# Global tokens in row-by-batch order, and the last output block in two column halves

## The chip, the cores and the metric

The kernel runs on one core of a Trainium2 chip. The metric is the device time of one execution in microseconds (us). Before the change three runs took 361.5, 361.63 and 361.71 us; their median is 361.63 us.

## The reference

Attention with a window, and a gated product behind it, for 8 batches of 8 heads, 512 local and 32 global tokens, head size 64 (so D = 512 columns). All is float32.

```python
out_g = softmax(scale * q_g @ [k_g, k_l].T) @ [v_g, v_l]            # 32 global tokens see all 544
out_l = softmax([scale * q_l @ k_g.T, band(scale * q_l @ k_l.T)]) @ [v_g, v_l]   # |i - j| <= 32
x = concat([out_g, out_l], tokens), heads side by side              # (8, 544, 512)
gate = sigmoid(causal convolution of x over tokens, 5 taps for each column)
out = ((gate * (x @ w_val)) @ w_out)                                # (8, 544, 512)
```

## The kernel before

Attention works on 32 units, each a batch and a pair of heads (`NU`, 128 columns of x). Its results stand transposed: 128 columns of x on the partitions, tokens along the free dimension. For the local tokens each batch has four such tiles of 512 tokens. The global tokens of all 8 batches are collected in `xgT` ([128, 4 column tiles, 8 batches, 4 + 32 tokens]; the four extra places hold zeros, for the causal taps) and are worked on once, at the very end, as one block of 8 x 32 = 256 tokens.

The function `moe` does the gated product: first product `g1` (x by `w_val`, for each of four output tiles e over four input tiles t), `gv` (times the gate, on DVE), `gh` and `gl` (the value split in a rounded high part and a rest, for float32 precision from three fast products), and second product `g2` (by `w_out`), which turns the result round: 128 tokens on the partitions, 512 columns in one PSUM bank. Each of `g1` and `g2` issues three matmuls for a step (high x high, high x low, low x high). `ob` copies a finished bank to SBUF and `st` stores it. `moe` is called for the eight batches (keys 0 to 7) and last with key `g` for the global tokens; there `g2` has two blocks r = 0, 1 of 128 tokens.

Before the call with key `g`, `wg_part` makes its inputs for each column tile from `xgT`, on DVE: `high` (a cast, `gxh`), `low` (a subtraction, `gxl`) and `conv` (`gconv`: one product with the first tap, then four scalar_tensor_tensor steps). They write the tiles `xgh`, `xgl` and `gateg`, each 128 x 256, through the views `hv`, `lv` and `acc`. Then `sigg` takes the sigmoid of the four gates on ACT.

Every task's place in its engine's queue is fixed by the table `ORDER`, written out by hand; a `Plan` gives the tasks their PSUM banks (the number behind @ in the table). The table ends

```
... g2.g.0.3 g2.g.1.0@5 st.7.3 g2.g.1.1 ob.g.0 g2.g.1.2 st.g.0 g2.g.1.3 ob.g.1 st.g.1
```

A store with key `g` was four DMAs, one for each batch in the block (32 tokens by 512 columns, 64 KB), in turn on the queues of SP and ACT.

Of the kernel before, what the change touches and what calls it, by code (L numbers as in the profile page):

```python
# [8 lines left out]
F32 = mybir.dt.float32  # L9
# [8 lines left out]
B, H, SL, SG, D = 8, 8, 512, 32, 64  # L18
DM = H * D
KW = 5  # L20
P = 128
NDT = DM // P
NU = B * NDT
# [294 lines left out]
def attention_moe(ctx, tc, qk, vw, maskd, w_val, convT, w_out, out):  # L318
    nc = tc.nc
    V, A, G, T = nc.vector, nc.scalar, nc.gpsimd, nc.tensor  # L320

    cp = ctx.enter_context(tc.tile_pool(name="cp", bufs=1))
    sb = ctx.enter_context(tc.tile_pool(name="sb", bufs=2))
    ps = ctx.enter_context(tc.tile_pool(name="ps", bufs=1, space=PSUM))

    plan = Plan()
    psum = ps.tile([P, 8, SL], F32, name="psum")

    def bank(key):
        return psum[:, plan.at[key][0], :]  # L330
# [23 lines left out]
    wvh, wvl, woh, wol = (cp.tile([P, NDT, DM], F32R, name=n) for n in ("wvh", "wvl", "woh", "wol"))  # L354
# [46 lines left out]
    def copy(name, out, in_):  # L401
        eng = plan.tasks[name].eng
        if eng == "ACT":
            A.copy(out, in_)  # L404
        else:
            (V if eng == "DVE" else G).tensor_copy(out, in_)
# [3 lines left out]
    def on_pe(ins):  # L410
        last_pe[:] = [ins.ins]
# [291 lines left out]
    gates, xs_h, xs_l = {}, {}, {}  # L703
# [3 lines left out]
    def moe(key, n, x0, deps_x, deps_gate, before, store):  # L707

        box = {}
        last = before  # L710

        def g1(e, t):
            xh, xl = xs_h[x0 + t], xs_l[x0 + t]
            if t == 0:
                box["pv", e] = bank(f"g1.{key}.{e}")[:, :n]
            for q, (w, x) in enumerate(((wvh, xh), (wvh, xl), (wvl, xh))):
                on_pe(T.matmul(box["pv", e], w[:, e, t * P:t * P + P], x, start=(t == 0 and q == 0),  # L717
                         stop=(t == NDT - 1 and q == 2)))

        def gv(e):  # L720
            if e == 0:
                box["gh"] = sb.tile([P, NDT, n], F32R, tag="gh", name=f"gh{key}", bufs=1)
                box["gl"] = sb.tile([P, NDT, n], F32R, tag="gl", name=f"gl{key}", bufs=1)
            box["gv", e] = sb.tile([P, n], F32, tag="gv", name=f"gv{key}_{e}")
            V.tensor_tensor(out=box["gv", e], in0=box["pv", e], in1=gates[x0 + e], op=ALU.mult)

        def gh(e):
            copy(f"gh.{key}.{e}", box["gh"][:, e, :], box["gv", e])

        def gl(e):  # L730
            V.tensor_tensor(out=box["gl"][:, e, :], in0=box["gv", e], in1=box["gh"][:, e, :].bitcast(F32),
                            op=ALU.subtract)

        def g2(r, e):
            if e == 0:
                box["po", r] = bank(f"g2.{key}.{r}")
            rs = slice(r * P, r * P + P)
            for q, (g, w) in enumerate(((box["gh"], woh), (box["gh"], wol), (box["gl"], woh))):
                on_pe(T.matmul(box["po", r], g[:, e, rs], w[:, e, :], start=(e == 0 and q == 0),  # L739
                         stop=(e == NDT - 1 and q == 2)))  # L740

        def ob(r):
            box["ob", r] = sb.tile([P, DM], F32, tag="ob", name=f"ob{key}_{r}")
            if (key, r) == ("g", n // P - 1):
                A.copy(box["ob", r][:, :DM // 2], box["po", r][:, :DM // 2])
                V.tensor_copy(box["ob", r][:, DM // 2:], box["po", r][:, DM // 2:])
            else:
                copy(f"ob.{key}.{r}", box["ob", r], box["po", r])

        part = 693 if n == 512 else 356  # L750
        early = [f"pc{u}.{KW - 1}" for u in range(NPC)] if key == 0 else []
        for e in range(NDT):
            for t in range(NDT):
                name = f"g1.{key}.{e}.{t}"
                plan.add(name, "PE", part, lambda e=e, t=t: g1(e, t), [last, f"w{e}"] + deps_x(t) + early,
                         take=[("bank", name[:-2])] if t == 0 else [],
                         give=[("xh", x0 + t), ("xl", x0 + t)] if e == NDT - 1 else [])
                last = name
            plan.add(f"gv.{key}.{e}", "DVE", 601 if n == 512 else 334, lambda e=e: gv(e),
                     [last] + deps_gate(e) + ([f"gv.{key}.{e - 1}"] if e else []),  # L760
                     take=[("gv", f"{key}.{e}")] + ([("g", key)] if e == 0 else []),
                     give=[("bank", f"g1.{key}.{e}"), ("gate", x0 + e)])
            plan.add(f"gh.{key}.{e}", (("ACT", 520 if n == 512 else 385), ("DVE", 335 if n == 512 else 205)), 0, lambda e=e: gh(e),
                     [f"gv.{key}.{e}"], lock=True)
            plan.add(f"gl.{key}.{e}", "DVE", 600 if n == 512 else 338, lambda e=e: gl(e), [f"gh.{key}.{e}"], 
                     give=[("gv", f"{key}.{e}")], lock=True)
        for r in range(n // P):
            for e in range(NDT):
                name = f"g2.{key}.{r}.{e}"
                plan.add(name, "PE", 682, lambda r=r, e=e: g2(r, e),  # L770
                         [last, f"gl.{key}.{e}", f"w{NDT + e}"], take=[("bank", name[:-2])] if e == 0 else [],
                         give=[("g", key)] if (r, e) == (n // P - 1, NDT - 1) else [])
                last = name
            plan.add(f"ob.{key}.{r}", *(("ACT", 350) if (key, r) == ("g", n // P - 1) else ((("ACT", 470), ("DVE", 600)), 0)), lambda r=r: ob(r), [last], take=[("ob", name[3:-2])],
                     give=[("bank", name[:-2])])
            plan.add(f"st.{key}.{r}", "ACT", 800 if key == "g" else 400, lambda r=r: store(r, box["ob", r]), [f"ob.{key}.{r}"])
            plan.add(f"sd.{key}.{r}", "DMA", 620, lambda: None, [f"st.{key}.{r}"], give=[("ob", f"{key}.{r}")])
        return last

    def wg_part(dt):  # L780

        n = B * SG
        src = xgT[:, dt]
        hv, lv, acc = (h[NU + dt].rearrange("p (b q) -> p b q", b=B) for h in (xs_h, xs_l, gates))

        def high():
            V.tensor_copy(hv, src[:, :, KW - 1:])

        def low():
            V.tensor_tensor(out=lv, in0=src[:, :, KW - 1:], in1=hv.bitcast(F32), op=ALU.subtract)  # L790

        def conv():
            V.tensor_scalar(out=acc, in0=src[:, :, 0:SG], scalar1=cw[:, dt, 0:1], scalar2=None, op0=ALU.mult)
            for k in range(1, KW):
                V.scalar_tensor_tensor(out=acc, in0=src[:, :, k:k + SG], scalar=cw[:, dt, k:k + 1], in1=acc,
                                       op0=ALU.mult, op1=ALU.add)

        return high, low, conv
# [40 lines left out]
    for b in range(B):  # L839
# [4 lines left out]
        for h in range(2):  # L844
            n = f"{b}.{h}"
# [16 lines left out]
    for u in range(NU):  # L862
        b, dt = divmod(u, NDT)
# [47 lines left out]
    for b in range(B):  # L911
        units = range(4 * b, 4 * b + 4)
        for u in units:
            plan.add(f"sig{u}", "ACT", 530, lambda u=u: sigmoid(gates[u]),
                     [f"fix{v}" if v < NHF else f"conv{v}.{KW - 2}" for v in units] + ([f"sig{u - 1}"] if u % 4 else []))
        last = moe(b, SL, 4 * b, lambda t, b=b: [f"xl{4 * b + t}"], lambda e, b=b: [f"sig{4 * b + e}"], last,
                   lambda r, o, b=b: A.dma_start(out[b, SG + r * P:SG + r * P + P, :], o))

    def open_g():
        n = B * SG  # L920
        for dt in range(NDT):
            xs_h[NU + dt] = sb.tile([P, n], F32R, tag="xh", name=f"xgh{dt}", bufs=NX)
            xs_l[NU + dt] = sb.tile([P, n], F32R, tag="xl", name=f"xgl{dt}", bufs=NX)
            gates[NU + dt] = sb.tile([P, n], F32, tag="gate", name=f"gateg{dt}", bufs=NX)
        gp.extend(wg_part(dt) for dt in range(NDT))
# [8 lines left out]
    plan.add("sigg", "ACT", 1250, lambda: [sigmoid(gates[NU + dt]) for dt in range(NDT)],  # L934
             [f"gconv{dt}" for dt in range(NDT)])

    def store_g(r, o):
        for s in range(P // SG):
            (A if s % 2 else nc.sync).dma_start(out[r * (P // SG) + s, 0:SG, :], o[s * SG:s * SG + SG, :])

    moe("g", B * SG, NU, lambda t: [f"gxl{t}"], lambda e: ["sigg"], last, store_g)

    with tc.manual_schedule():
# [91 lines left out]
```

## Time and profile before

| | |
|---|---|
| time, median of 3 runs | 361.63 us |
| the profiled execution's own time | 361.64 us |
| its span, from the first to the last instruction | 359.9 us |
| mean granted TensorE clock | 0.994 |
| busy: PE / DVE / ACT | 349.9 / 315.3 / 254.3 us |
| DMA traffic | 66.73 MB, 185 GB/s over the span |

Times in the views count from the start of the span. PE is the matmul engine, DVE the vector engine, ACT the scalar engine; SPq and ACTq are the queues on which SP and ACT issue DMAs. 1.74 us of the execution's time lie outside the span.

### The profile page before, as it was taken

To read this page: it belongs to the slowest core of one execution; us is meant where nothing else is said; L and a number is where in the kernel's file an instruction comes from. 1 tells how busy PE (TensorE), PEld (TensorE's weight loads), DVE (VectorE), ACT (ScalarE), POOL (GpSimd) and SP (SyncE) were. 2 spreads that over 40 slices of the span, in tenths; PEclk is the share of its full clock that TensorE was granted. 3 is DMA by queue.
4 is the path that set the end of the run, shared out by engine and by line. 5 is a ranking of instruction groups with operands and counts; after the bars stand their busy time and mean duration, and the time that the engine had idled before them with its cause. 6 is when DMAs were issued, how large, how long until landed. Compare 5 with 4: busy or idle time off the path is not lost.

```text
span 359.9 us, 14810 instructions
## 1 busy us (share of the span) xinstructions
PE 349.9 (97%) x6331; PEld 280.0 (78%) x6331; DVE 315.3 (88%) x1085; ACT 254.3 (71%) x652; POOL 0.8 (0%) x7
## 2 busy tenths in 40 slices
PE   8899999899999999999999999999999999999995
PEld 4666687778787888788878877888878888888894
DVE  4899999999989899899899997989599696988981
ACT  3899999897897688987788566776659458523131
POOL 0000000000000000000000000000000000000000
PEclk9899999999999999999999999999999999999999
DMA  7995947695675734925666482823854101000223
GB/s 280 400 362 166 359 156 279 209 402 193 226 235 199 276 104 108 391 102 171 221 241 237 159 277 104 262 67 132 283 165 173 62 2 51 13 29 36 112 87 87
DMA packets 17249, 66.73 MB, mean 185 GB/s; under 512 B 1952, under 2 KB 4000, under 8 KB 17184
## 3 DMA queue, kind: packets, MB, share of 16 engines
q1 hardware_dynamic: 12240, 57.12, 45.2%
q10 hardware_dynamic: 4944, 8.67, 6.6%
q8 instruction: 49, 0.80, 0.9%
q14 instruction: 16, 0.13, 0.1%
HBM read 56.87 MB, written 8.91 MB: 183 GB/s over the span
## 4 chain that ended last, share of the span: by engine, by line
PE 81%; ACT 8%; DMA 5%; DVE 3%; issue 1%; SPq 1%; ACTq 0%; DVEq 0%
PE psum L717 25%; PE psum L739 23%; PE psum L603 7%; PE psum L567 7%; PE psum L592 7%; PE psum L632 4%; DMA v<-in_vw_dram 3%; PE psum L531 3%; DMA out_dram<-ob 2%; ACT pm L586 2%; PE psum L493 2%; ACT xs L624 2%; PE psum L511 1%; DVE gate L668 1%; ACT xc L404 1%
## 5 line engine op out<-in xcount | busy, mean ns | idle before, releaser
L586 ACT ACTIVATE pm<-pm,mx 128x128 f32<-128x128 f32 x256 | 80.9, 407 | 25.8 <-DVE mx L579 22.5
L668 DVE SCALAR_TENSOR_TENSOR gate<-xc,cw,gate 128x512 f32<-128x512 f32 x120 | 87.7, 745 | 1.1 <-ACT gate L397 0.4
L579 DVE CUSTOM_DVE_ANT_0 pm<-psum,mask 128x128 f32<-128x128 f32 x256 | 57.4, 285 | 5.2 <-PE psum L567 5.2
L717 PE MATMUL psum<-xh,wvh 128*128 128x512 f32 x128 | 53.8, 421 | 0.0
L739 PE MATMUL psum<-woh,gh 128*128 128x512 f32 x128 | 53.0, 414 | 0.0
L717 PE MATMUL psum<-xl,wvh 128*128 128x512 f32 x128 | 50.6, 396 | 0.0
L717 PE MATMUL psum<-xh,wvl 128*128 128x512 f32 x128 | 50.5, 395 | 0.0
L739 PE MATMUL psum<-woh,gl 128*128 128x512 f32 x128 | 50.2, 392 | 0.0
L739 PE MATMUL psum<-wol,gh 128*128 128x512 f32 x128 | 50.0, 391 | 0.0
L404 ACT COPY pts<-psum 128x512 f32<-128x512 f32 x49 | 28.6, 601 | 16.0 <-PE psum L592 16.0
L592 PE MATMUL psum<-ident,pm 128*128 128x128 f32 x256 | 38.0, 278 | 0.6 <-ACT pm L586 0.3
L567 PE MATMUL psum<-qk 64*32 64x128 f32 x2048 | 38.1, 281 | 0.5 <-ACT pm L586 0.4
L603 PEld LDWEIGHTS psum<-v,pts 128*32 128x32 f32 x2048 | 31.1, 111 | 8.3 <-issue 4.7
L567 PEld LDWEIGHTS psum<-qk 64*32 64x32 f32 x2048 | 30.3, 108 | 8.5 <-issue 3.6
L592 PEld LDWEIGHTS psum<-ident,pm 128*128 128x128 f32 x256 | 29.6, 140 | 9.1 <-ACT pm L586 2.7
L603 PE MATMUL psum<-v,pts 128*32 128x65 f32 x2048 | 34.9, 224 | 1.4 <-DMA v<-in_vw_dram 1.2
L717 PEld LDWEIGHTS psum<-xh,wvl 128*128 128x128 f32 x128 | 24.0, 188 | 5.6 <-issue 0.2
L739 PEld LDWEIGHTS psum<-woh,gl 128*128 128x128 f32 x128 | 24.0, 188 | 5.3
L717 PEld LDWEIGHTS psum<-xh,wvh 128*128 128x128 f32 x128 | 24.3, 190 | 4.5 <-DVE xl L664 0.2
L717 PEld LDWEIGHTS psum<-xl,wvh 128*128 128x128 f32 x128 | 24.2, 189 | 4.1 <-issue 0.2
L739 PEld LDWEIGHTS psum<-woh,gh 128*128 128x128 f32 x128 | 24.2, 189 | 4.0 <-issue 0.2
L739 PEld LDWEIGHTS psum<-wol,gh 128*128 128x128 f32 x128 | 24.2, 189 | 3.9
(111 smaller groups left out, 554.0 us busy)
## 6 DMA issues: line engine op xcount, KB each, us to landing
v<-in_vw_dram SPq DMA_DIRECT2D x32, 975.0 KB, 6.7
qk<-in_qk_dram SPq DMA_DIRECT2D x32, 624.0 KB, 5.0
out_dram<-ob ACTq DMA_DIRECT2D x32, 256.0 KB, 2.2
wraw<-in_w_val_dram SPq DMA_DIRECT2D x4, 512.0 KB, 12.3
wraw<-in_w_out_dram SPq DMA_DIRECT2D x4, 512.0 KB, 4.1
mask<-in_mask_dram SPq DMA_DIRECT2D x1, 256.0 KB, 4.6
out_dram<-obg SPq DMA_DIRECT2D x4, 64.0 KB, 1.7
out_dram<-obg ACTq DMA_DIRECT2D x4, 64.0 KB, 2.0
```

Of the source, the lines that this page charges most:

```text
L404: A.copy(out, in_)
L493: on_pe(T.matmul(s[h][SG * c:SG * c + SG, cols], qkt[rows, SL + SG * h:SL + SG * h + SG], keys, start=True, stop=True))
L531: on_pe(T.matmul(ag[SG * c:SG * c + SG, :], pgt[:k, s, SG * c:SG * c + SG], vt[:k, w, h, :], start=(n == 0), stop=(n == len(steps) - 1)))
L567: on_pe(T.matmul((sx, sy)[h][32 * j:32 * j + 32, i, :], qkt[rows, 32 * m:32 * m + 32], qkt[rows, k0:k0 + P], start=True, stop=True))
L579: V.tensor_tensor_reduce(out=pm[:, h, i, :], in0=s[:, i, :], in1=mask[:, i, :], op0=ALU.add, op1=ALU.min, scale=-SCALE, scalar=3.0e38, acc ...
L586: A.activation(out=pm[:, h, i, :], in_=pm[:, h, i, :], func=AF.Exp, bias=mx[:, c:c + 1], scale=-1.0)
L592: on_pe(T.transpose(pt[:, i, :], pm[:, h, i, :], ident))
L603: on_pe(T.matmul(ax[32 * j:32 * j + 32, h, E1 * i:E1 * i + E1], pts[:, h, i, 32 * j:32 * j + 32], vt[:, block_win(4 * i + j), h, :], start ...
L632: on_pe(T.transpose(xt[:, P * i:P * i + P], xs[:, i].rearrange("p h d -> p (h d)"), ident))
L668: V.scalar_tensor_tensor(out=acc, in0=xc[:, k:k + SL], scalar=cw[:, u % NDT, k:k + 1], in1=acc, op0=ALU.mult, op1=ALU.add)
L717: on_pe(T.matmul(box["pv", e], w[:, e, t * P:t * P + P], x, start=(t == 0 and q == 0), stop=(t == NDT - 1 and q == 2)))
L739: on_pe(T.matmul(box["po", r], g[:, e, rs], w[:, e, :], start=(e == 0 and q == 0), stop=(e == NDT - 1 and q == 2)))
```

## The change

Two things are changed together, both for key `g`.

The 256 global tokens are numbered token by token with the batches inside (q, b) and no longer batch by batch (b, q). The tiles `xgh`, `xgl` and `gateg` keep their size, but DVE now goes through them in steps of 8 elements (32 bytes), since `xgT` is still read batch by batch. One block r of 128 rows of the second product then holds tokens 16r to 16r + 15 of all eight batches, and one DMA of three dimensions (16 tokens, 8 batches, columns) stores it.

The last block (r = 1) is computed by `g2_halves` in two halves of 256 columns, each in its own bank: all twelve products of columns 0 to 255, then all twelve of columns 256 to 511. The first half is copied by DVE to a tile `obg_first` and stored from SP when it is done, the second by ACT and stored from SP. Block r = 0 is stored by one DMA on ACT's queue.

```diff
+        def g2_halves(r, e):
+            if e % (NDT // 2) == 0:
+                used = [plan.at[f"g2.{key}.{i}"][0] for i in (r - 1, r)]
+                spare = next(n for n in (f"g1.{key}.{i}" for i in range(NDT)) if plan.at[n][0] not in used)
+                box["half", e * 2 // NDT] = bank(spare if e else f"g2.{key}.{r}")
+            c, rs = e * 2 // NDT, slice(r * P, r * P + P)
+            for k in range(e * 2 % NDT, e * 2 % NDT + 2):
+                for q, (g, w) in enumerate(((box["gh"], woh), (box["gh"], wol), (box["gl"], woh))):
+                    on_pe(T.matmul(box["half", c][:, :DM // 2], g[:, k, rs], w[:, k, c * DM // 2:(c + 1) * DM // 2],
+                             start=(k == 0 and q == 0), stop=(k == NDT - 1 and q == 2)))
+            if (c, k) == (0, NDT - 1):
+                o = sb.tile([P, DM // 2], F32, tag="gv", name="obg_first")
+                V.tensor_copy(o, box["half", 0][:, :DM // 2])
+                store(r, o, 0)
+
         def g2(r, e):
+            if (key, r) == ("g", n // P - 1):
+                g2_halves(r, e)
+                return
...
         def ob(r):
-            box["ob", r] = sb.tile([P, DM], F32, tag="ob", name=f"ob{key}_{r}")
-            if (key, r) == ("g", n // P - 1):
-                A.copy(box["ob", r][:, :DM // 2], box["po", r][:, :DM // 2])
-                V.tensor_copy(box["ob", r][:, DM // 2:], box["po", r][:, DM // 2:])
+            last_part = (key, r) == ("g", n // P - 1)
+            o = box["ob", r] = sb.tile([P, DM // 2 if last_part else DM], F32, tag="ob", name=f"ob{key}_{r}")
+            if last_part:
+                A.copy(o, box["half", 1][:, :DM // 2])
...
-        hv, lv, acc = (h[NU + dt].rearrange("p (b q) -> p b q", b=B) for h in (xs_h, xs_l, gates))
+        hv, lv, acc = (h[NU + dt].rearrange("p (q b) -> p b q", b=B) for h in (xs_h, xs_l, gates))
...
-    def store_g(r, o):
-        for s in range(P // SG):
-            (A if s % 2 else nc.sync).dma_start(out[r * (P // SG) + s, 0:SG, :], o[s * SG:s * SG + SG, :])
+    def store_g(r, o, c=1):
+        cols = slice(0, DM) if r == 0 else slice(c * DM // 2, (c + 1) * DM // 2)
+        (nc.sync if r else A).dma_start(out[:, P // B * r:P // B * r + P // B, cols].rearrange("b q d -> q b d"), o)
```

The table `ORDER` is the same. Three places show what now stands in the queues; names are those of the program with buffer numbers. First the end of ACT's queue, from the copy of block r = 0 on (`obg`), before (-) and after (+):

```order
-L404 COPY obg_5952<-psum 128x512
-L939 DMA out_dram<-obg_5952 32x512 x2
-L745 COPY obg_5964<-psum 128x256
-L939 DMA out_dram<-obg_5964 32x512 x2
-L1030 UNCONDITIONAL_BRANCH
+L404 COPY obg_5961<-psum 128x512
+L957 DMA out_dram<-obg_5961 16x8x512
+L764 COPY obg_5976<-psum 128x256
+L1048 UNCONDITIONAL_BRANCH
```

ACT issues one DMA where there were four, and none behind its last copy. At the end of SP's queue, behind the last loads of v, the stores of `obg` stand so:

```order
 L416 DMA v_5000<-in_vw_dram 128x1950
-L939 DMA out_dram<-obg_5952 32x512 x2
-L939 DMA out_dram<-obg_5964 32x512 x2
-L1030 UNCONDITIONAL_BRANCH
+L957 DMA out_dram<-obg_first 16x8x256
+L957 DMA out_dram<-obg_5976 16x8x256
+L1048 UNCONDITIONAL_BRANCH
```

SP issues the store of the first half and then that of the second. On DVE no instruction moves in the queue; the last conversions for the global tokens (`gconv2` in the table's words is one product and four scalar_tensor_tensor steps; `gconv3` and `gconv1` follow) now go through 8 x 32 elements where one row of 256 stood, and the last copy writes `obg_first`. The stretch ahead of the gated product, after the change:

```order
L808 TENSOR_TENSOR xgl_5733<-xgT,xgh_5732 128x8x32
L811 TENSOR_SCALAR gateg_5734<-xgT,cw 128x8x32
L813 SCALAR_TENSOR_TENSOR gateg_5734<-xgT,cw,gateg_5734 128x8x32 x4
L811 TENSOR_SCALAR gateg_5728<-xgT,cw 128x8x32
L813 SCALAR_TENSOR_TENSOR gateg_5728<-xgT,cw,gateg_5728 128x8x32 x4
L406 COPY ob_0_5867<-psum 128x512
L725 TENSOR_TENSOR gvg_5889<-psum,gateg_5725 128x256
```

The gated product of the global tokens (`gvg`) stands directly behind these conversions and one copy. On PE the twelve matmuls of 128 x 512 that ended the program are 24 of 128 x 256, each with its own load of weights.

More of the change, by code (lines that the diff above doesn't have):

```diff
@@ L742, in ob @@
         def ob(r):
-            box["ob", r] = sb.tile([P, DM], F32, tag="ob", name=f"ob{key}_{r}")
-            if (key, r) == ("g", n // P - 1):
-                A.copy(box["ob", r][:, :DM // 2], box["po", r][:, :DM // 2])
-                V.tensor_copy(box["ob", r][:, DM // 2:], box["po", r][:, DM // 2:])
+            last_part = (key, r) == ("g", n // P - 1)
+            o = box["ob", r] = sb.tile([P, DM // 2 if last_part else DM], F32, tag="ob", name=f"ob{key}_{r}")
+            if last_part:
+                A.copy(o, box["half", 1][:, :DM // 2])
             else:
-                copy(f"ob.{key}.{r}", box["ob", r], box["po", r])
+                copy(f"ob.{key}.{r}", o, box["po", r])
         part = 693 if n == 512 else 356
```

## The prediction

> **What bounds the kernel now.** I read the page's busy times first, then the chain of waits over the last 30 us, then the timeline of the end, then the stores' landing times. The page, and the chain (start, length, work):
>
> ```profile
> PE 349.9 (97%) x6331; PEld 280.0 (78%) x6331; DVE 315.3 (88%) x1085; ACT 254.3 (71%) x652; POOL 0.8 (0%) x7
> 329.77 3.93 PE psum L717 x17
> 333.70 10.88 PE psum L739 x48
> 344.58 5.69 PE psum L717 x48
> 350.27 5.46 PE psum L739 x24
> 355.73 0.02 issue
> 355.75 0.38 ACT obg L745
> 356.13 0.02 issue
> 356.16 0.42 DVE obg L746
> ```
>
> PE is the bound, and it runs without a gap to 355.73. Behind it comes a tail of 4.2 us in which only the last block is on its way: ACT copies one half, DVE then the other, and four stores go out. These are the rows of the tail:
>
> ```profile
> 355.33 0.39 PE L739 MATMUL psum<-woh,glg 128*128 128x512 f32 x1
> 355.75 0.37 ACT L745 COPY obg<-psum 128x256 f32<-128x256 f32 x1 [2.13 <-PE psum L739]
> 356.16 0.42 DVE L746 COPY obg<-psum 128x256 f32<-128x256 f32 x1 [4.64 <-ACT obg L745]
> 356.61 0.78 SPq L939 DMA_DIRECT2D out_dram<-obg  x2
> 356.62 0.85 ACTq L939 DMA_DIRECT2D out_dram<-obg  x2
> L939 SPq DMA_DIRECT2D out_dram<-obg x2: 315/364/414, 356.6 to 357.0; - x2
> L939 ACTq DMA_DIRECT2D out_dram<-obg x2: 375/408/441, 356.6 to 357.0; - x2
> DMA to landing us min/median/max: 1.6/1.9/2.0
> out_dram<-obg SPq DMA_DIRECT2D x4, 64.0 KB, 1.7
> out_dram<-obg ACTq DMA_DIRECT2D x4, 64.0 KB, 2.0
> SPq L1030 <- DMA out_dram<-obg: 1.4, 2, 1.2
> ```
>
> The two copies don't overlap: DVE waited for ACT, since both write one tile. Then each queue issues two stores one behind the other. ACT's second one starts at 356.62 + 0.85 - 0.44 = 357.03 and lands 2.0 later, at 359.03; SP's starts at 356.98 and lands by 1.7, at 358.7. So ACT's second store ends the program's work, SP waits for it (last row), and 0.87 us of closing steps make the span of 359.9. The profiled execution took 361.64, the median of the runs is 361.63: I count from 361.64 and need no correction.
>
> **The change, part by part.**
>
> *The last block on PE.* Twelve matmuls of 512 columns become 24 of 256. The chain prices both: 24 of L739 take 5.46, so 227 ns each; 48 of L717, which have 256 columns and a weight load each, take 5.69, so 118.5 ns each. 12 x 0.2275 = 2.73 becomes 24 x 0.1185 = 2.84: +0.11 on the path. The twelve start at 355.33 - 11 x 0.2275 = 352.83, so the last of the 24 would start at 352.83 + 23 x 0.1185 = 355.56 and, at the 0.28 that the L717 form takes (row further down), end at 355.84.
>
> *The copies.* ACT's copy stays on the path: 355.84 + 0.02 (issue, as in the chain) = 355.86, and 0.37 later it is 356.23. DVE's copy leaves it, with the issue gap ahead: -0.44. It moves to the first half, which is complete 12 matmuls earlier, at 352.83 + 11 x 0.1185 + 0.28 = 354.41; DVE has nothing to do then (it sat idle for 4.64 ahead of its copy), so it copies until about 354.9 and nothing waits for it but SP's first store, out by 355.3.
>
> *The stores of the last block.* SP issues the second half's store when ACT is done, at 356.26. Nothing stands ahead of it: the first half's store has left the queue 0.9 earlier. So the last issue moves from 357.03 to 356.26. Landing of such a store (128 pieces of 1 KB, 128 KB, SP's queue) is not in the trace. Its neighbours are SP's 64 KB at 1.7 (1.6 the least) and ACT's stores of 128 rows:
>
> ```profile
> L917 ACTq DMA_DIRECT2D out_dram<-ob x1: 339/339/339, 350.3 to 350.3; - x1
> DMA to landing us min/median/max: 2.0/2.0/2.0
> L917 ACTq DMA_DIRECT2D out_dram<-ob x1: 444/444/444, 346.9 to 346.9; - x1
> DMA to landing us min/median/max: 2.3/2.3/2.3
> ```
>
> 256 KB from a free queue took 2.0, right behind another store 2.3. I take 1.75, near SP's 64 KB, because it is the same queue and both have few bytes for each DMA engine; the ends are 1.6 and 2.3. Landing at 356.26 + 1.75 = 358.01 instead of 359.03 is -1.02, in which the +0.11 on PE is contained.
>
> *The store of block 0.* Four DMAs of 64 KB from 353.65 become one of 256 KB on ACT. At 2.0 to 2.3 it lands by 356.0, before the last store is issued, and ACT's queue is free 0.4 later at the latest, long before ACT's copy at 355.86. Cost 0; the cover is the second half's work on PE.
>
> *The new order of the tokens.* It adds no instruction, but 28 DVE instructions now write, and 20 of them also read, in steps of 32 bytes. These are they before, and the nearest rows for a strided access (raw weights in steps of 8 bytes beside a plain row; PSUM in steps of a few hundred bytes with 8 and 2 elements):
>
> ```profile
> L795 DVE SCALAR_TENSOR_TENSOR gateg<-xgT,cw,gateg 128x256 f32<-128x256 f32 x16 | 7.8, 485 | 0.6
> L790 DVE TENSOR_TENSOR xgl<-xgT,xgh 128x256 fp32r<-128x256 f32 x4 | 1.6, 418 | 0.0
> L793 DVE TENSOR_SCALAR gateg<-xgT,cw 128x256 f32<-128x256 f32 x4 | 1.4, 347 | 0.0
> L787 DVE CAST xgh<-xgT 128x256 fp32r<-128x256 f32 x4 | 1.1, 287 | 0.0
> L668 DVE SCALAR_TENSOR_TENSOR gate<-xc,cw,gate 128x512 f32<-128x512 f32 x120 | 87.7, 745 | 1.1 <-ACT gate L397 0.4
> L375 DVE TENSOR_SCALAR wraw<-wa 128x512 int32<-128x512 int32 x8 | 3.4, 428 | 0.0
> L371 DVE TENSOR_SCALAR wa<-wa 128x512 int32<-128x512 int32 x8 | 3.3, 414 | 0.0
> L612 DVE TENSOR_SCALAR mx<-psum 128x8 f32<-128x8 f32 x32 | 5.2, 161 | 6.1 <-PE psum L603 5.4 <-ACT xc L404 0.4
> L536 DVE TENSOR_SCALAR gd<-psum 128x2 f32<-128x2 f32 x8 | 1.2, 154 | 0.6 <-PE psum L531 0.6
> ```
>
> Writing in steps of 8 bytes costs 14 ns over 512 elements. Reading PSUM with every element far from the last costs (161 - 154) / 6 = 1.2 ns an element, about the plain step of (745 - 485) / 256 = 1.02 ns. Neither shows a second step per element, so the low end is 0 (below it nothing: the elements to process are the same). The high end is one more step per element, 0.26 us for each of the 28 instructions; no row shows SBUF in steps of 32 bytes. How much of a delay is hidden stands in these rows:
>
> ```profile
> 333.74 0.69 DVE L725 TENSOR_TENSOR gv<-psum,gate 128x512 f32<-128x512 f32 x1 [0.44 <-PE psum L717]
> 345.80 0.68 DVE L406 COPY ob<-psum 128x512 f32<-128x512 f32 x1
> 346.40 0.42 DVE L725 TENSOR_TENSOR gvg<-psum,gateg 128x256 f32<-128x256 f32 x1
> 347.53 0.42 DVE L725 TENSOR_TENSOR gvg<-psum,gateg 128x256 f32<-128x256 f32 x1 [0.72 <-PE psum L717]
> 348.69 0.28 PE L717 MATMUL psum<-xgh,wvh 128*128 128x256 f32 x1
> ```
>
> Five of the 28 stand ahead of the row at 333.74, where DVE waits 0.44 for PE anyway. The other 23 run without a pause until the copy at 345.80. The second `gvg` at 347.53 waits 0.72 for PE; it frees its bank at 347.95, and PE's fourth group of `g1`, which takes that bank, starts at 348.69, 0.74 later. With x for the cost of one instruction, PE stalls by 28x - 0.44 - 0.72 - 0.74 = 28x - 1.90. It stalls by nothing while x is under 0.068 us, a quarter of a step. I take the low end, where the two nearest rows stand, and so a cost of 0.
>
> [...]
>
> **Sum.** 361.64 - 1.02 = 360.6. With a landing of 1.6 it is 360.5, with 2.3 it is 361.2.
>
> **Rivals.**
>
> *DVE becomes the bound ahead of the global product (slower).* If each element costs one more step, 28 x 0.26 - 1.90 = 5.4 us of stall at the fourth group of `g1`: 360.6 + 5.4 = 366.0. It eats the gain from 28x - 1.90 = 1.02 on, that is x = 0.104 us, 0.4 of a step. For it: every strided access changes its place by 32 bytes, which no row covers, and DVE is busy without a break just there. Against it: the PSUM reads of L612, and that a lesser loss stays hidden: if only the 8 casts and one-tensor products fell back to the pace of L795 (485 - 347 = 0.14 each), that is 1.1 in all, under 1.90. [...]
>
> *The single store eats the gain.* One queue now brings 128 pieces of 1 KB where two queues brought 64 pieces of 2 KB each. From a landing of 2.05 us on, less than 0.2% is left; at 2.75 nothing is. That gives 360.9 to 361.6. For it: the 2.3 of a store behind another one, since the first half's store is in front. Against it: that store is 1.3 us ahead, and 256 KB landed in 2.0.
>
> *The change doesn't do what it says.* SP's second store could wait for the first to land, if both count on one semaphore: 354.95 + 1.75 = 356.70 instead of 356.26, so 361.06. In the program they count on different ones, so I give it little and put it with the case before.
>
> **How the numbers follow.** A measurement of this kernel can tell about 0.2%, 0.72 us, from no change; faster means below 360.9. The forecast has a chance of 0.60, with a range of its own from 360.3 to 361.2: 0.50 of it below 360.9, 0.10 within 0.2%. DVE as the bound has 0.30, 0.02 of it small enough to end within 0.2%, 0.28 slower, and most of that near the full step at 366.0, because the step comes whole or not at all. The store's cases have 0.10: 0.08 within 0.2%, 0.02 slower. So faster 0.50, same 0.20, slower 0.30. A range that stops short of the full step would leave out more than 2 in 10, so it goes from 360.3 to 366.1.
>
> **What would show it.** Right: 128 x 8 x 32 instructions on DVE within 20 ns of 485, 418, 347 and 287; no gap on PE between 344 and the end; the last ACT copy ending about 0.4 after the last matmul, and the last SP issue directly behind it, with a landing of 1.6 to 2.0; DVE's copy of the first half inside PE's last 1.4 us. Wrong: the conversions at 0.6 us and more, with PE waiting for `gvg`; a landing over 2.05; or a wait of SP for a DMA ahead of its last store. The prediction rests most on the first of these.

## The result, and the profile after

The changed kernel takes 366.75 us (median of four runs, 365.97 to 367.27) where the kernel before takes 361.67 beside it: a ratio of 1.0135, 95% interval 1.0111 to 1.0158. I had forecast 360.6 us, with a range up to 366.1. It is slower, by the cost that the first rival named (DVE's conversions), and slower than that rival's price. Below, five executions were over 1.5% above the fastest of their kernel (two of the changed kernel on another chip, three in experiments): the ratios leave them out, the medians keep them.

The profiled execution took 366.8 us with a span of 365.0. These are the 28 conversions in the view by line and shape of the changed kernel (last column but one: mean ns of one):

```profile
L813 DVE SCALAR_TENSOR_TENSOR gateg<-xgT,cw,gateg 128x256 f32<-128x256 f32 x16 | 11.6, 724 | 0.6
L808 DVE TENSOR_TENSOR xgl<-xgT,xgh 128x256 fp32r<-128x256 f32 x4 | 2.6, 678 | 0.0
L811 DVE TENSOR_SCALAR gateg<-xgT,cw 128x256 f32<-128x256 f32 x4 | 1.8, 460 | 0.0
L805 DVE CAST xgh<-xgT 128x256 fp32r<-128x256 f32 x4 | 1.5, 425 | 0.0
```

They were at 485, 418, 347 and 287. The timeline of DVE shows where the conversions end, that of PE what that does:

```profile
347.52 2.82 DVE L813 SCALAR_TENSOR_TENSOR gateg<-xgT,cw,gateg 128x256 f32<-128x256 f32 x4
350.26 0.69 DVE L406 COPY ob<-psum 128x512 f32<-128x512 f32 x1
```

```profile
344.17 0.28 PE L717 MATMUL psum<-xgh,wvh 128*128 128x256 f32 x1
346.90 0.28 PE L717 MATMUL psum<-xgh,wvl 128*128 128x256 f32 x1
...
351.00 0.38 PE L717 MATMUL psum<-xgh,wvh 128*128 128x256 f32 x1 [3.82 <-DVE ob L406]
351.22 0.28 PE L717 MATMUL psum<-xgl,wvh 128*128 128x256 f32 x1
...
352.47 0.41 PE L717 MATMUL psum<-xgl,wvh 128*128 128x256 f32 x1
352.68 0.41 PE L717 MATMUL psum<-xgh,wvl 128*128 128x256 f32 x1
...
355.45 0.40 PE L757 MATMUL psum<-woh,ghg 128*128 128x512 f32 x1
```

PE stands still for 3.8 us after the second group of the global `g1`, waiting for a copy on DVE (`ob` of batch 7). Then it starts at its usual pace of 118 ns, and from 352 on takes 213 ns for the same matmuls. The windows of the same trace give the granted clock (a row has the window, its length, PE's busy time and instructions, the clock, the DMA engines' busy share and GB/s):

```profile
347.00:351.00 4.00, 0.18 (x3) 1.00 0.00 0
351.00:352.00 1.00, 1.00 (x8) 1.00 0.19 70
352.00:355.40 3.40, 3.40 (x18) 0.51 0.57 211
355.45:358.20 2.75, 2.75 (x13) 1.00 0.28 101
```

So 3.4 us run at half clock. In the kernel before, the third group and the global `g2` start here:

```profile
347.27 0.27 PE L717 MATMUL psum<-xgh,wvh 128*128 128x256 f32 x1
350.11 0.39 PE L739 MATMUL psum<-woh,ghg 128*128 128x512 f32 x1
```

And the changed tail, with the stores and their landing times:

```profile
359.86 0.42 DVE L746 COPY obg_first<-psum 128x256 f32<-128x256 f32 x1 [2.99 <-PE psum L742]
360.98 0.28 PE L742 MATMUL psum<-woh,glg 128*128 128x256 f32 x1
361.30 0.37 ACT L764 COPY obg<-psum 128x256 f32<-128x256 f32 x1 [2.28 <-PE psum L742]
361.69 0.55 SPq L957 DMA_DIRECT2D out_dram<-obg  x1
```

```profile
out_dram<-obg ACTq DMA_DIRECT2D x1, 256.0 KB, 3.0
out_dram<-obg_first SPq DMA_DIRECT2D x1, 128.0 KB, 2.4
out_dram<-obg SPq DMA_DIRECT2D x1, 128.0 KB, 2.3
```

From the first matmul of the global `g1` to the end of the span it is 15.48 us before (344.42 to 359.9) and 20.83 after (344.17 to 365.0). The 5.35 us come from four pieces:

| piece | before | after | |
|---|---|---|---|
| to the start of the third group | 2.85 | 6.83 | +3.98 |
| third and fourth group | 2.84 | 4.45 | +1.61 |
| global `g2`, to the end of the last matmul | 5.61 | 5.81 | +0.20 |
| tail, to the end of the span | 4.18 | 3.74 | -0.44 |

I use this stretch to compare traces below, because what lies ahead of it differs between executions of one kernel (in the two traces of the halves alone, below, the stretch begins at 341.88 and at 345.32).

### The profile page after: what moved, and what is told of

The parts are those of the page before. It is cut to its first block, busy times and chain, and to the rows that moved or that the text cites. A ratio compares the mean times of both kernels' runs of the same rounds, so it can differ in the third digit from the quotient of the medians.

```text
span 365.0 us, 14827 instructions
## 1 busy us (share of the span) xinstructions
PE 350.0 (96%) x6343; PEld 281.3 (77%) x6343; DVE 320.8 (88%) x1085; ACT 254.7 (70%) x652; POOL 0.9 (0%) x7
## 4 chain that ended last, share of the span: by engine, by line
PE 85%; DVE 6%; DMA 3%; ACT 3%; issue 2%; SPq 1%; ACTq 0%; DVEq 0%
PE psum L717 24%; PE psum L757 22%; PE psum L603 8%; PE psum L592 8%; PE psum L567 7%; PE psum L632 4%; DVE gateg L813 3%; PE psum L531 3%; DMA v<-in_vw_dram 3%; PE psum L693 2%; PE psum L493 2%; PE psum L511 2%; PE psum L513 1%; ACT xs L624 1%; PE psum L742 1%
## 5 line engine op out<-in xcount | busy, mean ns | idle before, releaser
L567 PE MATMUL psum<-qk 64*32 64x128 f32 x2048 | 37.0, 277 | 0.6 <-ACT pm L586 0.6
L567 PEld LDWEIGHTS psum<-qk 64*32 64x32 f32 x2048 | 29.5, 107 | 8.0 <-issue 3.2
```

Of the source, the lines that this page charges most:

```text
L567: on_pe(T.matmul((sx, sy)[h][32 * j:32 * j + 32, i, :], qkt[rows, 32 * m:32 * m + 32], qkt[rows, k0:k0 + P], start=True, stop=True))
```

## The experiments

**The halves without the new order** (tokens batch by batch again, each half stored by four DMAs):

```diff
-... rearrange("p (q b) -> p b q", b=B)
+... rearrange("p (b q) -> p b q", b=B)
-        (nc.sync if r else A).dma_start(out[:, P // B * r:..., cols].rearrange("b q d -> q b d"), o)
+        for s in range(P // SG):
+            (A if s % 2 else nc.sync).dma_start(out[r * (P // SG) + s, 0:SG, cols], o[s * SG:s * SG + SG, :])
```

The stores of the first half are issued behind those of block 0.

> The change without the new order of tokens: the last block in two halves of columns, each in its own bank and tile, but tokens batch by batch as before and every half stored by four DMAs of 32 rows x 256 columns, in turn on SP and ACT. Theory A (the 5 us come from DVE's steps of 32 bytes alone): the conversions are back at 485, 418, 347 and 287 ns, PE has no gap, PE's last block is 0.11 longer and DVE's copy is off the tail (-0.44); with issues and landings as before about 361.3 us (361.1 to 361.6). Theory B (the halves or what stands around them cost it): 364 us or more.

> The halves without the new order once more, since the executions of its first comparison differed by 5 us among themselves. In its trace the stretch from the first matmul of the global g1 to the end was 0.46 us shorter than before (14.86 from the chain's row against 15.32). If that is what it is worth, the ratio is 0.9987, with 0.9975 to 1.0; if the executions before and after that stretch differ too, it stays open.

The medians were 362.84 (before 362.24 on that chip; ratio 0.9991, interval 0.9955 to 1.0027) and, the second time, 361.48 (before 361.68; 0.9991, 0.9962 to 1.0019). The 5 us are gone, so theory B falls: its 364 us would be 0.6% over before, outside both intervals. The conversions are back at 485, 416, 347 and 286 ns. In the second trace the chain of waits and the last stores read:

```profile
345.48 5.69 PE psum L717 x48
351.17 2.72 PE psum L757 x12
353.89 2.88 PE psum L742 x24
356.78 0.02 issue
356.80 0.37 ACT obg L764
```

```profile
out_dram<-obg SPq DMA_DIRECT2D x2, 32.0 KB, 1.5
out_dram<-obg ACTq DMA_DIRECT2D x2, 32.0 KB, 1.7
```

The 48 matmuls run without a gap, and the stretch is 15.02 us (341.88 to 356.9) in the first trace and 14.98 (345.32 to 360.3) in the second, 0.46 and 0.50 under before. Whether that shortens the whole execution the timed runs don't decide: both intervals hold 0.9987 as well as 1.

**The order without the halves** (the kernel before with the new view, one store for each block):

> The kernel before with the new order of tokens alone (conversions in steps of 32 bytes, one store for each block of 128 rows, the last one from SP); the last block is one bank and one tile as before, copied by ACT and then DVE. Theory A (DVE's steps of 32 bytes hold PE's third group of g1): conversions near 724, 678, 460 and 425 ns, 3.8 us of idle PE behind the second group and some 3.4 us at half clock, so the stretch from the first matmul of the global g1 to the end is 5.3 us longer than before plus what the single store of 256 KB loses in the tail (2.9 us to landing against 0.4 + 2.0): about 6 us, 367.5 us where before is 361.7. Theory B (the halves cost part of it): clearly less than 5 us over before.

367.23 us against 361.68, ratio 1.018 (1.0134 to 1.0226). Its conversions take 720, 687, 456 and 410 ns, and PE waits 3.8 us for the same copy:

```profile
L795 DVE SCALAR_TENSOR_TENSOR gateg<-xgT,cw,gateg 128x256 f32<-128x256 f32 x16 | 11.5, 720 | 0.6
353.56 0.58 PE L717 MATMUL psum<-xgh,wvh 128*128 128x256 f32 x1 [3.79 <-DVE ob L406]
```

In its profiled execution the stretch is 21.83 us (346.77 to 368.6), 6.35 over before; about 6 were expected. The order, with the steps that it makes DVE take, carries the loss alone.

**Fast conversions in the new order**: everything as changed, but `xgT` itself lies token by token, so that a conversion reads and writes 256 elements in a row (the diff leaves out the other accesses to `xgT`, which follow its new shape).

```diff
-    xgT = cp.tile([P, NDT, B, KW - 1 + SG], F32, name="xgT")
+    xgT = cp.tile([P, NDT, KW - 1 + SG, B], F32, name="xgT")
-        hv, lv, acc = (... rearrange("p (q b) -> p b q", b=B) ...)      # src[:, :, k:k + SG]
+        hv, lv, acc = (... rearrange("p (q b) -> p q b", b=B) ...)      # src[:, k:k + SG, :]
```

> The changed kernel whole, but xgT itself lies token by token with the batches inside ([128, 4, 36, 8]), so that the 28 conversions read and write 256 elements in a row, and only the 8 copies into xgT (128 x 128 each) write in steps of 32 bytes. Theory A: conversions back at 485, 418, 347 and 287 ns or a little less, no gap on PE, no stretch at half clock; the tail keeps the changed kernel's -0.43 and PE its +0.11, so about 361.3 us (361.0 to 361.6). Theory B (order and stores of the global tokens cost time even where DVE is fast): 364 us or more. If the 8 copies now hold somebody: 361.7 to 363.

362.72 us, ratio 1.0016 (0.9986 to 1.0046), and no gap on PE. The conversions are back at 485, 417, 346 and 286 ns:

```profile
L813 DVE SCALAR_TENSOR_TENSOR gateg<-xgT,cw,gateg 128x256 f32<-128x256 f32 x16 | 7.8, 485 | 0.6
```

The stretch is 15.16 us (346.14 to 361.3), 0.32 under before, against the 0.3 expected. The whole time was to be 0.1% under before; the interval holds that, and also a small loss as in the third case of the expectation. So neither the order of the rows in memory nor their stores cost the 5 us, only the steps in which DVE went through them. What now goes in steps of 32 bytes are the copies from PSUM into `xgT` (and reads of at most four elements for the causal taps). They take, in this kernel and then in the one before:

```profile
L404 ACT COPY xgT<-psum 128x128 f32<-128x128 f32 x5 | 2.0, 399 | 2.6 <-DVE ob L406 2.1 <-PE psum L548 0.4
L406 DVE COPY xgT<-psum 128x128 f32<-128x128 f32 x3 | 1.2, 400 | 1.4 <-PE psum L548 1.4
```

```profile
L404 ACT COPY xgT<-psum 128x128 f32<-128x128 f32 x5 | 1.4, 279 | 2.5 <-DVE ob L406 2.1 <-PE psum L548 0.4
L406 DVE COPY xgT<-psum 128x128 f32<-128x128 f32 x3 | 0.9, 287 | 1.4 <-PE psum L548 1.4
```

Here only the write is strided, and it costs 120 ns on ACT and 113 on DVE for 128 elements, 0.9 ns for each. (In the traces with plain writes ACT's mean lies between 260 and 287 ns, so its price is less sure than DVE's.)

**How large a step is free.** The kernel before, with conversions that write `(x l)` for l = 2 or 4, and read 256 elements of `xgT` in a row instead of the tokens. So they leave out the right results, and only their times count:

```diff
-... rearrange("p (b q) -> p b q", b=B)
+... rearrange("p (x l) -> p l x", l=2)     # 8 bytes; l=4: 16 bytes
```

> The kernel before with the 28 conversions writing (and reading their own results) in steps of 8 bytes; they read xgT as 256 elements in a row, so the values and the order of the global tokens are others. [...] Rival (any step beyond one element costs, the more the larger): 530 to 600 ns for the scalar_tensor_tensor step.

> The same in steps of 16 bytes. [...]

The view by line and shape, first of steps of 8 bytes, then of 16:

```profile
L796 DVE SCALAR_TENSOR_TENSOR gateg<-xgT,cw,gateg 128x256 f32<-128x256 f32 x16 | 7.8, 486 | 0.6
L788 DVE CAST xgh<-xgT 128x256 fp32r<-128x256 f32 x4 | 1.1, 286 | 0.0
```

```profile
L796 DVE SCALAR_TENSOR_TENSOR gateg<-xgT,cw,gateg 128x256 f32<-128x256 f32 x16 | 11.0, 685 | 0.6
L791 DVE TENSOR_TENSOR xgl<-xgT,xgh 128x256 fp32r<-128x256 f32 x4 | 2.4, 624 | 0.0
L794 DVE TENSOR_SCALAR gateg<-xgT,cw 128x256 f32<-128x256 f32 x4 | 1.8, 448 | 0.0
L788 DVE CAST xgh<-xgT 128x256 fp32r<-128x256 f32 x4 | 1.4, 390 | 0.0
```

8 bytes cost next to nothing (1 ns on 485, at most 2 in the other three forms), so the rival's 530 to 600 ns did not come. 16 bytes cost 200 ns, about four fifths of what 32 bytes cost (239); in the other forms it is 75 to 89%. So most of the price, 200 of the 239 ns, comes in one jump between 8 and 16 bytes, and the other 39 between 16 and 32. Each took one execution: 361.71 and 365.86 us.

**Who holds PE.** The changed kernel with batch 7's copy `ob.7.0` on ACT:

```diff
-... ob.7.0:DVE g1.g.1.1 ob.7.2 ...
+... ob.7.0 g1.g.1.1 ob.7.2 ...
```

> The changed kernel with the copy of batch 7's first output block (ob.7.0) on ACT instead of on DVE behind the conversions. Theory A (PE's third group waits for the bank that this copy frees): the third group starts without a wait; PE then waits ahead of the fourth group for the gated product gv of the second, about 2.9 us, from 348.4 to 351.3; with the clock still halved behind it 365.7 us, without 364.1. Rival (the third group waits for the conversions in another way): no change, 366.7 us.

365.54 us, ratio 1.0071 (1.0038 to 1.0103). The timeline of PE and the granted clock behind the gap:

```profile
347.71 0.28 PE L717 MATMUL psum<-xgh,wvh 128*128 128x256 f32 x1
...
348.66 0.28 PE L717 MATMUL psum<-xgh,wvl 128*128 128x256 f32 x1
351.72 0.58 PE L717 MATMUL psum<-xgh,wvh 128*128 128x256 f32 x1 [2.78 <-DVE gvg L725]
```

```profile
351.70:354.60 2.90, 2.88 (x13) 0.50 0.57 213
```

The third group now runs through and the fourth waits 2.8 us for `gvg`. The holder was the bank of `ob.7.0`, and behind it stands the one I had named, of `gvg`. In this profiled execution (366.1 us) the clock halves after the shorter gap as well. The timed runs gain more than expected for that case: 365.7 was 4.0 over before, and the ratio is 2.6 us over before on this chip (1.4 to 3.7), nearer to the 2.4 expected without the half clock. Of the eight executions in the ratio three had a mean clock of 1.000 and took 362.4 to 365.0 us, five had 0.989 to 0.995 and took 365.1 to 366.1. This suggests that behind this gap the clock falls in some executions only; it doesn't show it.

**Whether the half clock follows from the gap.** 16 matmuls of weights by weights into an unused bank where PE stood idle:

```diff
+            if (key, e, t) == ("g", 2, 0):
+                for _ in range(16):
+                    on_pe(T.matmul(psum[:, 6, :], woh[:, 0, :P], woh[:, 1, :], start=True, stop=True))
```

> The changed kernel with 16 more matmuls of 512 columns (of weights by weights, into a bank that nobody uses) ahead of the third group of g1 of the global tokens, where PE stood idle for 3.8 us. Theory A (the half clock from 352.0 to 355.4 follows from the idle time): no stretch with a granted clock near 0.5, the 24 matmuls behind at 118 ns each, about 1.6 us less, 365.1 us. Theory C (that stretch is slow because of the two stores of 256 KB that move in it): it stays slow, 366.7 us.

> The changed kernel once more, beside pe_busy_again on one chip, since executions on different chips differ by up to 2 us. 1.3 to 1.4% over before; in its profile PE idle for 3.8 us ahead of the third group of the global g1, and a stretch with half the granted clock behind it.

> The changed kernel with the 16 idle-time matmuls, on the same chip. In the first trace the 24 matmuls behind them took 2.95 us against 4.45 and the stretch from the first matmul of the global g1 to the end was 1.26 us shorter. Theory A (the half clock belongs to every execution): 1.2 to 1.5 us less than the changed kernel on this chip. Rival (it comes only in some executions, the profiled one among them, or the 16 matmuls cost as much elsewhere): within 0.5 us of it.

The first comparison gave 366.75 us, ratio 1.0129 (1.0084 to 1.0173): not theory A's 365.1 but the 366.7 of theory C, so by its time alone C would stand. The traces speak against it. In the chain of waits the 24 matmuls behind the gap take, in the second comparison, with the 16 matmuls and then in the changed kernel itself on the same chip:

```profile
351.63 3.12 PE psum L720 x24
```

```profile
351.76 5.49 PE psum L717 x24
```

At 118 ns each, with 0.28 for the last, 24 take 3.0: 3.12 us is nearly the full pace. In all four traces this holds: a stretch at half pace behind 3.8 us of idle time, none where the time was filled, though two stores of 256 KB are issued there in both (on that chip at 351.61 and 351.98 with the filled gap, at 351.73 and 352.11 without). So theory C falls. The stretch is 19.57 and 19.51 us with the filled gap, 20.83 and 21.65 without. The timed runs don't show that gain: on that chip 1.0126 of before (1.0085 to 1.0167) with the filled gap and 1.0103 (1.0055 to 1.0152) without, where the four executions of the changed kernel in the ratio reach from 364.68 to 368.52 us. (That executions on different chips differ by up to 2 us was my estimate. The kernel before has medians of 362.24, 361.68 and 362.47 us on the three chips of the experiments, and on each of them alone its executions differ by 3.0 to 5.3 us.) So the traces show that the half clock costs 1.3 to 2.1 us in the stretch of a profiled execution. How many of the other executions have it, and how long, is open. The mean clock of each execution is on record: 0.985 to 0.995 in all ten of the changed kernel, 0.995 to 1.0 in all ten with the filled gap, and 3.4 us at half clock lower the mean by 0.005. That fits a half clock in every execution of the changed kernel, but in the kernel before the mean also lies between 0.993 and 1.0, so it doesn't say where the clock fell.

## Why the prediction was wrong

**DVE's steps of 32 bytes: the step that failed.** I set their cost to 0 by two rows, raw weights in steps of 8 bytes (14 ns on 512) and PSUM reads far apart (1.2 ns an element). Both rows were read rightly and neither covered the case: 8 bytes lie below the jump, and the others read PSUM. The term was mis-sized from 0 to 16 x 239 + 4 x 260 + 4 x 113 + 4 x 138 ns = 5.9 us of DVE time; for each instruction that is 0.4 to 1.0 of the step that I had named as the high end (113 to 260 ns of 260). It came whole in one form only (`low`, 260) and in part in the others, where I had it whole or not at all. The first rival named the case, a place that changes by 32 bytes at each access, which no row covered, and I gave it half the forecast's chance (0.30 against 0.60). The experiments bear it out: 485 ns in a row and 486 at 8 bytes, but 685 at 16 and 724 at 32.

**How much of the delay is hidden.** My 28x - 1.90 gives 5.87 - 1.90 = 3.97 us, and the third group started 3.98 late. That is partly luck: I had the holder wrong. PE's third group takes bank 4, which the copy of `ob.7.0` at 345.80 frees, right behind the conversions; in the trace before, that copy ended at 346.48 and the group started at 347.27, with 0.79 to spare. I looked only at the bank that `gvg` frees for the fourth group. Counted from the first matmul of the global `g1`, the copy starts at 1.38 before and at 6.09 after, 4.71 later, and 0.79 of that was to spare: 3.92, which leaves 0.06. So three errors nearly cancel: the slack behind the conversions was 0.79, where I had 1.46 (0.72 + 0.74); the first five conversions, 0.93 us by their prices, held up nothing, where I had 0.44 to hide them (`gv` starts 10.68 ahead of that matmul before and after); and the other 23 cost 4.71, where their prices add up to 4.93.

**The half clock: missing from the rival.** The rival's 366.0 had the stall without its consequence. The third and fourth group took another 1.61 us, since the granted clock was 0.51 from 352.0 to 355.4, behind the gap.

**PE's last block** was right: 24 matmuls take 2.88 in the chain, 2.84 expected.

**The copies** were right: DVE copied the first half at 359.86, while PE worked on the second, and ACT's copy ended at 361.67, 0.41 after the last matmul.

**The single store: wrong size.** The last issue stood directly behind ACT's copy, as forecast, but it landed after 2.3 us, not 1.75, the upper end of my bounds. Block 0's store took 3.0, so it was still on its way when the last one was issued (359.04 + 3.0 = 362.04, against 361.69), which I had excluded; whether that delayed the last one is not shown. Issue itself takes 0.55 to 0.66 us on its queue, where a plain store of 128 rows took 0.34 (0.44 right behind another). The tail gained 0.44 instead of 1.13: 0.55 of the difference is the landing, and about 0.14 lies between the landing and the end of the span (1.01 where it was 0.87). With fast conversions the whole stretch gains 0.32 where I had 1.02, so that even without the rival the change would have ended within 0.2%. That is the second rival, and it was true too. The halves alone, with four small plain stores each, have the shortest stretch of all (14.98 and 15.02 us against 15.16), so in these traces the new order gained nothing even where DVE is fast.

**The numbers.** The range ended at 366.1 because it stopped at the rival's price of 366.0. Against that price the stall was 1.4 shorter (3.98 instead of 5.4), the half clock added 1.6, and the gain at the end was 0.8 smaller (0.44 - 0.20 = 0.24 instead of 1.02). That makes 367.0; the profiled execution took 366.8, mostly because its stretch began 0.25 earlier. I had also taken 0.2% as what a comparison can tell; the intervals of the experiments reach 0.3 to 0.5% to either side, so that the forecast gain of 0.3% would hardly have been clear of them.

## What to carry to other kernels

A new order of data can be paid for by whoever writes and reads it in steps (here 239 ns more on 485 in steps of 32 bytes, and 1 in steps of 8): count the bytes between consecutive elements on each engine, and move the steps to the smallest instructions (here 8 copies of 128 elements instead of 28 conversions of 256 that hold PE; that the 8 cost nothing anywhere is not shown). When a step has no row in the trace, its price is not that of the nearest row but open between rows on both sides of the jump. Price a stall of PE with what follows it: the holder is the last reader of each bank ahead, and the work behind a gap can run at half clock, as it did here behind 2.8 and 3.8 us (granted clock 0.50 and 0.51), but not behind 3.1.

## What the runs showed of the hardware

- In the traces with steps of 16 and of 32 bytes in SBUF (the 32 in the changed kernel) the steps cost 0.8 to 1.0 ns for each element in two-operand instructions of DVE (200 to 260 ns on 256) and 0.4 to 0.5 in its casts and one-tensor products (101 to 138 on 256). Writes from PSUM in steps of 32 bytes cost 0.9, on DVE as on ACT (113 and 120 on 128). The two-operand ones also read one operand in steps, the others only write so; the runs don't separate this from the kind of instruction. In the experiment with steps of 8 bytes these instructions paid at most 2 ns on 256.
- The scalar_tensor_tensor step in steps of 32 bytes took longer beside a busy PE: in the changed kernel four took 2.82 us while PE was idle and 3.13 just before. With the gap filled by matmuls the same four took 3.11 and 3.02 in the two traces, and the mean over all sixteen was 740 and 738 ns instead of 724. In steps of 16 bytes there was no such difference (2.83 beside an idle PE, 2.84 to 2.87 otherwise), and with elements in a row the mean was 485 in every trace.
- Behind gaps of 3.8 us (three traces) and of 2.8 (one) PE took 213 ns for matmuls that otherwise take 118; the granted clock there was 0.51 in the changed kernel and 0.50 behind the gap of 2.8. The slow pace ended 4.45 us behind the gap in the first trace of the changed kernel, 5.3 behind it in the one on the other chip, and 3.4 behind it with the order alone. Behind a gap of 3.1 us with steps of 16 bytes the clock stayed at 1.00:

```profile
351.33 0.39 PE L717 MATMUL psum<-xgh,wvh 128*128 128x256 f32 x1 [3.10 <-DVE ob L406]
```

```profile
351.33:354.40 3.07, 3.07 (x25) 1.00 0.46 171
```

  So the length of a gap alone doesn't decide it. The moment differs too: in the first trace of the changed kernel the slow pace began 1.05 us behind the gap, in the other three the first matmul behind the gap was slow already (0.58 us instead of 0.38). What decides it was not tried.
- A store with three dimensions in memory (16 tokens x 8 batches x 512 columns) landed 2.9 to 3.0 us after its issue, a plain one of the same 256 KB and the same 2 KB rows after 2.0 from a free queue (the kernel before, at 350.3). The reason beyond the longer issue was not tried.
